# Cluster masks made in two ways, and a separate step for turning the row maxima, in a routed-attention and feed-forward kernel

## The chip, the core and the metric

The kernel runs on one core of a Trainium2 chip. A core has a matrix engine (TensorE, PE in the profile; its weight loads are the row PEld), a vector engine (VectorE, DVE), an activation engine (ScalarE, ACT), a general engine (GpSimd, POOL) and DMA queues. Here transfers are issued by the SyncE queue (SP) and, for one load, by ScalarE's own queue. Matrix products land in PSUM, which the tile framework hands out as banks; vector and scalar engines read them from there. Each engine takes its own instructions in order and waits for others by semaphores.

The metric is the device time of one execution in microseconds (us), the median of several runs.

## What is computed

Two blocks follow each other. In the first, each query and each key of a head is assigned to the nearest of 16 centroids (by cosine), and a query attends only to keys of its own cluster. The second is a feed-forward block with the activation `h * erf(softplus(h))`.

```python
# B, H, S, D = 4, 8, 768, 64 ; 16 clusters ; d_model 512, d_ff 2048 ; all float32
q_n = q / (norm(q) + 1e-6); k_n = ...; c_n = ...
q_assign = argmax(q_n @ c_n.T)            # the first maximum wins
k_assign = argmax(k_n @ c_n.T)
mask   = q_assign[..., :, None] == k_assign[..., None, :]
scores = where(mask, q @ k.T / sqrt(D), -1e9)
attn   = softmax(scores)
x      = attn @ v                          # then (B,H,S,D) -> (B*S, H*D)
h      = x @ w_in
out    = (h * erf(softplus(h))) @ w_out
```

## The kernel before

Heads are worked on in pairs: 16 pairs, four to a batch. Pair `p` has 12 score blocks of 128 keys by 384 queries for both heads; a block is called a slot below. While pair `p` goes through its slots, pair `p+1` is prepared beside it by a generator, `aside(p+1)`, which is advanced by single steps. The steps of a pair are: transpose q and k (VectorE); products with the centroids (`psim`) and half of the bf16 copies; the cluster choice (`hot`); the other bf16 copies; the masks; and then, for each half of the queries, a bf16 pass over all scores for the row maxima (`sm`, reduced to `nmx`), their minimum (`nm`), and the turning of these maxima into one row per head.

The masks are not a separate operand. They are rows of the bf16 operands `qm` and `km` that carry q and k as well, so that a second, bf16 product adds to the float32 scores a very negative number wherever clusters differ; the turned maxima are one more row of `qm`.

```python
# route(p), after the centroid products
ve.transpose(out=sims, in_=psim)
ve.reduce_max(out=mx, in_=sim, axis=AX.X)
ve.tensor_tensor(out=hot..., in0=sim, in1=mx (broadcast), op=ALU.is_equal)   # bf16, ties possible
ve.transpose(out=hotT, in_=hot)
yield
vectors("k")                       # bf16 copies of k, ScalarE
yield
won = ps_x.tile([P, HW], F32, name="won", tag="x")
te.matmul(won, lhsT=first, rhs=hotT, start=True, stop=True)   # subtracts earlier winners: first maximum only
for half in range(2):
    for e in range(2):
        if half == 0:
            ve.tensor_scalar(out=low["q"][r, e, cols], in0=won[g], scalar1=own[g, e:e+1], scalar2=0.0, op0=ALU.mult, op1=ALU.max)
        else:
            ae.activation(out=low["q"][r, e, cols], in_=won[g], func=ACT.Relu, scale=own[g, e:e+1])
        ae.activation(out=low["k"][r, e, cols], in_=won[g'], func=ACT.Identity, bias=nbig[g'], scale=BIG)
yield
# ... shift(p): six steps of sm and nmx, the last of them with the minimum, then
ve.tensor_reduce(out=nm, in_=nmx[:, :, ts], axis=AX.X, op=ALU.min)
yield
te.transpose(out=pn, in_=nm..., identity=identb)
ae.copy(out=nmT, in_=pn)
for e in range(2):
    for t in range(HJ):            # 6 rows, one transfer each, all on the SyncE queue
        nc.sync.dma_start(out=st["qm"][r:r+1, e, ...], in_=nmT[e*HJ+t : e*HJ+t+1])
yield
```

`ps_x`, the pool of PSUM banks that nearly everything shares (`psim`, `won`, `sm`, `pn`, `av`, `psum`, `hp`, `po`), has four buffers; the scores have two of their own.

The weights come in as 8-byte numbers and are converted on the chip, in 32 steps of two halves each: `convert()` is advanced by `prepare(n)`. The first half of a step has a maximum on VectorE and a sign pass on ScalarE; the second half has a shift on VectorE, an addition on GpSimd, and `split`, two ScalarE passes that open the next step.

The first batch goes by a fixed plan, one row for each of a pair's 12 slots:

```python
# (own steps, next pair's steps before the scores, after the scores, prepare)
plan = (
    (1,0,1,0), (1,0,2,0), (1,0,1,0), (1,0,0,0), (0,0,1,1), (0,0,1,1),
    (0,0,2,1), (0,0,2,1), (0,1,0,2), (0,1,0,0), (0,0,2,1), (0,0,1,1),
)
advance(0, 3); prepare(2); advance(0, NJ + 1); prepare(1); advance(0, HJ)   # before slot 0
for slot in range(48):
    advance(p, own_steps); advance(p + 1, before); scores([slot])
    ...divide, advance(p + 1, after), prepare(ops), accumulate(slot - 1), attend(slot - 2)
    if slot >= 45: pump(...)               # from here feed-forward products fill in
```

Engines keep program order up to slot 45. In the later batches scores go two slots at a time, the feed-forward products of the batch before (`hp`, `po`) are pumped between them, and the next pair's steps are taken at the places listed in `ASIDE`.

Of the kernel before, what the change touches and what calls it, by code (L numbers as in the profile page):

```python
# [8 lines left out]
F32 = mybir.dt.float32  # L9
BF16 = mybir.dt.bfloat16  # L10
# [3 lines left out]
ALU = mybir.AluOpType  # L14
ACT = mybir.ActivationFunctionType
AX = mybir.AxisListType
PSUM = bass.MemoryType.PSUM

P = 128
B, H, S, D = 4, 8, 768, 64  # L20
C = 16
NJ = S // P
Q = 32
NB = S // Q
HW = S // 2
HJ = NJ // 2
HP = H // 2
# [10 lines left out]
BIG = 2.0**60  # L38
FLOOR = 2.0**50
EPS = 2.0**-70  # L40
SH = 2 * C
# [2 lines left out]
SLOTS = 5  # L44


ASIDE = (*range(5), *range(8, 8 + 2 * NJ), 10 + 2 * NJ, 12 + 2 * NJ)
REST = 3
FIRST = 2 * NJ * HP - 3

# [18 lines left out]
def kernel(  # L69
# [10 lines left out]
    nc = tc.nc  # L80

    in_order = [True]
    te, ve, ae, ge = (
        InOrder(tc, e, in_order) for e in (nc.tensor, nc.vector, nc.scalar, nc.gpsimd)
    )
# [4 lines left out]
    const = pool("const", 1)  # L90
# [3 lines left out]
    routep = pool("routep", 1)  # L94
    small = pool("small", 2)
# [6 lines left out]
    ps_x = pool("ps_x", 4, space=PSUM)  # L102

    ident = const.tile([P, P], F32, name="ident")
    identb = const.tile([P, P], BF16, name="identb")
    minus = const.tile([P, D], F32, name="minus")
    first = const.tile([P, P], BF16, name="first")
    nbig = const.tile([P, 1], F32, name="nbig")
    ccT = const.tile([P, HP, 2 * C], F32, name="ccT")
# [2 lines left out]
    own = const.tile([P, 2], F32, name="own")  # L112
# [12 lines left out]
    pairs = {}  # L125
# [43 lines left out]
    for base, pattern, sign, op, fill in (  # L169
# [5 lines left out]
            out=first, in_=first, compare_op=op, fill=fill, base=base, pattern=pattern,  # L175
# [93 lines left out]
    for it in range(2):  # L269
# [4 lines left out]
            out=twice, in0=ss, scalar=inv, in1=norm, op0=ALU.mult, op1=ALU.add  # L274
# [3 lines left out]
            out=norm, in0=twice, scalar1=0.5, scalar2=(1e-6 if it else 0.0),  # L278
            op0=ALU.mult, op1=ALU.add,
# [11 lines left out]
    def route(p):  # L291
        st = pairs[p]
        low = lows[p % 2]
        for e in range(2 if p > 1 else 0):
            r = e * D + SH
            nc.sync.dma_start(out=low["q"][r : r + 1, e], in_=low["q"][r + 1 : r + 2, e])
        for nm in "qk":
            raw = rowp.tile([P, S], F32, name=nm + "T")
            ve.transpose(out=raw, in_=st.pop(nm).rearrange("p n t -> p (n t)"))
            st[nm + "T"], st[nm + "m"] = raw, low[nm]  # L300
        load_qk(p + 1)
        yield

        psim = ps_x.tile([P, HW], F32, name="psim", tag="x")
        for g in range(4):
            te.matmul(
                psim[2 * C * g : 2 * C * (g + 1)], lhsT=ccT[:, p % HP],
                rhs=st["qk"[g // 2] + "T"][:, (g % 2) * HW : (g % 2 + 1) * HW],
                start=True, stop=True,
            )  # L310

        def vectors(nm):
            for e in range(2):
                ae.copy(
                    out=low[nm][(1 - e) * D : (2 - e) * D, e], in_=st[nm + "T"][e * D : (e + 1) * D]
                )

        vectors("q")
        yield

        sims = routep.tile([P, HW], F32, name="sims")
        ve.transpose(out=sims, in_=psim)
        n = HW // C
        sim = sims.rearrange("p (g c) -> p g c", c=C)
        mx = routep.tile([P, n], F32, name="mx")
        ve.reduce_max(out=mx, in_=sim, axis=AX.X)
        hot = routep.tile([P, HW], BF16, name="hot")
        ve.tensor_tensor(
            out=hot.rearrange("p (g c) -> p g c", c=C), in0=sim,
            in1=mx.unsqueeze(2).to_broadcast([P, n, C]), op=ALU.is_equal,  # L330
        )
        hotT = routep.tile([P, HW], BF16, name="hotT")
        ve.transpose(out=hotT, in_=hot)
        yield
        vectors("k")
        yield

        won = ps_x.tile([P, HW], F32, name="won", tag="x")
        te.matmul(won, lhsT=first, rhs=hotT, start=True, stop=True)

        for half in range(2):
            cols = slice(half * HW, (half + 1) * HW)
            for e in range(2):
                r = slice(e * D, e * D + Q)
                g = slice(half * Q, (half + 1) * Q)
                if half == 0:
                    ve.tensor_scalar(
                        out=low["q"][r, e, cols], in0=won[g], scalar1=own[g, e : e + 1], scalar2=0.0,
                        op0=ALU.mult, op1=ALU.max,
                    )  # L350
                else:
                    ae.activation(
                        out=low["q"][r, e, cols], in_=won[g], func=ACT.Relu, scale=own[g, e : e + 1]
                    )
                g = slice(D + half * Q, D + (half + 1) * Q)
                ae.activation(
                    out=low["k"][r, e, cols], in_=won[g], func=ACT.Identity, bias=nbig[g], scale=BIG
                )
        yield


# [1 line left out]
    def shift(p):  # L363


        st = pairs[p]
        nmx = maxima[p % 2]
        load(p, "v", v, vp)
        for h in range(2):
            ts = slice(h * HJ, (h + 1) * HJ)  # L370
            for t in range(h * HJ, (h + 1) * HJ):
                for half in range(2):
                    for e in range(2):
                        sm = ps_x.tile([P, HW], F32, name="sm", tag="x")
                        te.matmul(
                            sm, lhsT=st["qm"][:, e, t * P : (t + 1) * P],
                            rhs=st["km"][:, e, half * HW : (half + 1) * HW], start=True, stop=True,
                        )
                        ve.tensor_reduce(
                            out=nmx[:, e, t, half : half + 1], in_=sm, axis=AX.X, op=ALU.max, negate=True  # L380
                        )
                    if (t, half) != ((h + 1) * HJ - 1, 1):
                        yield
            nm = small.tile([P, 2, HJ], BF16, name="nm")
            ve.tensor_reduce(out=nm, in_=nmx[:, :, ts], axis=AX.X, op=ALU.min)
            yield
            pn = ps_x.tile([2 * HJ, P], BF16, name="pn", tag="x")
            te.transpose(out=pn, in_=nm.rearrange("p e t -> p (e t)"), identity=identb)
            nmT = small.tile([2 * HJ, P], BF16, name="nmT")
            ae.copy(out=nmT, in_=pn)  # L390
            for e in range(2):
                r = e * D + SH
                for t in range(HJ):
                    nc.sync.dma_start(
                        out=st["qm"][r : r + 1, e, h * HW + t * P : h * HW + (t + 1) * P],
                        in_=nmT[e * HJ + t : e * HJ + t + 1],
                    )
            yield

# [203 lines left out]
    def prepare(n):  # L605
        for _ in range(n):
            next(conv, None)
# [3 lines left out]
    def aside(p):  # L611
# [3 lines left out]


    plan = (
        (1, 0, 1, 0), (1, 0, 2, 0), (1, 0, 1, 0), (1, 0, 0, 0), (0, 0, 1, 1), (0, 0, 1, 1),
        (0, 0, 2, 1), (0, 0, 2, 1), (0, 1, 0, 2), (0, 1, 0, 0), (0, 0, 2, 1), (0, 0, 1, 1),
    )  # L620
    ready = {0: aside(0)}
    part = iter(())
# [1 line left out]
    def advance(p, n):  # L624
        for _ in range(n):
            next(ready[p])
# [5 lines left out]
    for e in range(2):  # L632
        ve.tensor_copy(
            out=ccT[e * D : (e + 1) * D, :, e * C : (e + 1) * C],
            in_=pct[e * D : (e + 1) * D].rearrange("d (r e c) -> d r e c", e=2, c=C)[:, :, e],
        )
    ve.tensor_copy(out=identb, in_=ident)
    ve.memset(minus, -1.0)
    ve.memset(nbig, -BIG)
    ve.memset(alleps, S * EPS)  # L640
    for t in maxima:
        ve.memset(t, FLOOR)

    for e in range(2):
        ve.reduce_sum(
            out=own[:, e : e + 1],
            in_=ident.rearrange("p (g x c) -> p x g c", x=2, c=C)[:, e], axis=AX.XY,
# [4 lines left out]
    advance(0, 3)  # L652
    prepare(2)
    advance(0, NJ + 1)
    prepare(1)
    advance(0, HJ)
    for slot in range(2 * NJ * HP):
        in_order[0] = slot < FIRST
        p, r = divmod(slot, 2 * NJ)
        if r == 0:  # L660
            ready[p + 1] = aside(p + 1)
        own_steps, before, after, ops = plan[r]
        advance(p, own_steps)
        advance(p + 1, before)
        scores([slot])
        if r % NJ == 2 and slot > 2:
            part = divide(slot - 3)
            next(part)
        advance(p + 1, after)
        if r % NJ == 3:  # L670
            next(part, None)
        if slot not in (FIRST - 1, FIRST):
            prepare(ops)
        if slot > 0:
            accumulate(slot - 1)
        if slot >= 2:
            attend(slot - 2)
        if slot >= FIRST:
            pump(4 * NFT * TB)
# [13 lines left out]
    for u in range(2 * NJ * HP, len(units), 2):  # L693
        p, half, j = units[u]
# [59 lines left out]
```

## Time and profile before

| | us |
|---|---|
| median of 3 runs (1229.11 to 1232.9) | 1229.4 |
| profiled span | 1227.9 |
| first exponential (slot 0) starts | 35.04 |
| exponential of slot 44 starts, the last before feed-forward products begin | 166.52 |
| PE busy (95% of the span) | 1162.6 |
| DVE busy (38%) | 471.8 |
| ACT busy (48%) | 589.4 |
| POOL busy (38%) | 460.8 |

The mean granted TensorE clock is 0.98 of full. "Busy" for PE counts overlapping, modelled ends of pipelined products, so 95% isn't 95% of the engine's peak; which stage is limited by what is read from the order of instructions and from the waits in that stage.

### The profile page before, as it was taken

To read this page: it belongs to the slowest core of one execution; us is meant where nothing else is said; L and a number is where in the kernel's file an instruction comes from. 1 tells how busy PE (TensorE), PEld (TensorE's weight loads), DVE (VectorE), ACT (ScalarE), POOL (GpSimd) and SP (SyncE) were. 2 spreads that over 40 slices of the span, in tenths; PEclk is the share of its full clock that TensorE was granted. 3 is DMA by queue.
4 is the path that set the end of the run, shared out by engine and by line. 5 is a ranking of instruction groups with operands and counts; after the bars stand their busy time and mean duration, and the time that the engine had idled before them with its cause. 6 is when DMAs were issued, how large, how long until landed. Compare 5 with 4: busy or idle time off the path is not lost.

```text
span 1227.9 us, 13280 instructions
## 1 busy us (share of the span) xinstructions
PE 1162.6 (95%) x4913; PEld 621.7 (51%) x4913; DVE 471.8 (38%) x887; ACT 589.4 (48%) x705; POOL 460.8 (38%) x466
## 2 busy tenths in 40 slices
PE   4888979899999989999999999999999999999998
PEld 1222236564444545465465455455456456576663
DVE  5677864443443442333243244343425112011121
ACT  4687776677333545183364455256264254032222
POOL 2477774445333433154243234234234343030200
PEclk8799999899999999999999999999999999999999
DMA  8544332122020201020200201002000000000000
GB/s 133 125 91 91 79 115 56 54 67 48 3 46 16 42 8 33 9 41 8 35 23 1 48 10 26 22 10 39 4 27 1 9 9 1 12 7 18 0 18 18
DMA packets 140753, 42.95 MB, mean 35 GB/s; under 512 B 133520, under 2 KB 133520, under 8 KB 140688
## 3 DMA queue, kind: packets, MB, share of 16 engines
q1 hardware_dynamic: 137552, 41.70, 15.4%
q10 hardware_dynamic: 3136, 0.39, 0.3%
q8 instruction: 39, 0.64, 0.2%
q14 instruction: 26, 0.21, 0.1%
HBM read 35.68 MB, written 6.29 MB: 34 GB/s over the span
## 4 chain that ended last, share of the span: by engine, by line
PE 73%; ACT 10%; DVE 7%; issue 7%; DMA 2%; POOL 1%; ACTq 0%; SPq 0%; DVEq 0%
PE po L60 25%; PE hp L60 22%; PE sc L60 13%; PE av L60 6%; PE sm L60 4%; ACT a_s L60 2%; ACT L60 2%; DVE nmx L60 2%; ACT km L60 1%; DVE den L60 1%; PE psim L60 1%; ACT inv L60 1%; DVE w_out L60 1%; ACT pr L60 1%; ACT qm L60 1%
## 5 line engine op out<-in xcount | busy, mean ns | idle before, releaser
L60 PE MATMUL hp<-xT,w_in 128*128 128x256 f32 x1536 | 388.0, 389 | 7.1 <-DVE xT L60 5.4
L60 PE MATMUL po<-w_out,g 128*128 128x512 f32 x768 | 368.8, 598 | 0.6 <-DVE den L60 0.6
L60 POOL TENSOR_TENSOR acc<-acc,pr 128x384 f32<-128x384 f32 x256 | 239.3, 965 | 313.3 <-ACT pr L60 313.3
L60 PEld LDWEIGHTS hp<-xT,w_in 128*128 128x128 f32 x1536 | 288.6, 193 | 130.1 <-issue 81.6
L60 ACT ACT_TABLE_LOAD x111 | 142.4, 1283 | 231.3 <-DVE g L60 129.8
L60 DVE TENSOR_REDUCE nmx<-sm 128x1 f32<-128x384 f32 x384 | 195.5, 549 | 134.7 <-PE sm L60 133.8
L60 ACT ACTIVATE pr<-sc 128x768 f32<-128x768 f32 x192 | 148.0, 806 | 164.6 <-PE sc L60 164.0
L60 PEld LDWEIGHTS po<-w_out,g 128*128 128x128 f32 x768 | 142.0, 190 | 106.5 <-issue 93.6
L60 PE MATMUL sc<-qT,kT 64*128 64x384 f32 x768 | 186.5, 532 | 3.7 <-ACT pr L60 3.6
L60 POOL TENSOR_TENSOR g<-a_s,g 128x512 f32<-128x512 f32 x88 | 109.8, 1279 | 203.5 <-ACT a_s L60 203.5
L60 DVE COPY g<-hp 128x512 f32<-128x512 f32 x96 | 65.9, 687 | 282.1 <-PE hp L60 282.1
L60 PE MATMUL av<-pr,in_v 128*64 128x386 f32 x768 | 142.0, 500 | 0.8 <-DVE nmx L60 0.8
L60 PE MATMUL sm<-km,qm 128*128 128x384 bf16 x384 | 106.3, 341 | 31.8 <-DVE nmx L60 14.1
L60 PEld LDWEIGHTS sc<-qT,kT 64*128 64x128 f32 x768 | 71.6, 189 | 83.6 <-issue 47.2
L60 POOL TENSOR_TENSOR acc<-pr,pr 128x384 f32<-128x384 f32 x64 | 64.3, 1026 | 106.1 <-ACT pr L60 106.1
L60 PEld LDWEIGHTS av<-pr,in_v 128*64 128x64 f32 x768 | 49.5, 137 | 90.4 <-issue 76.8
L60 PEld LDWEIGHTS <-qm 128*128 128x128 bf16 x384 | 35.4, 99 | 95.2 <-issue 83.7
L60 DVE SCALAR_TENSOR_TENSOR den<-psum,inv 128x384 f32<-128x384 f32 x32 | 17.8, 556 | 141.5 <-ACT inv L60 141.2
L60 ACT ACTIVATE a_s<-a_s 128x2048 f32<-128x2048 f32 (+3 forms) x48 | 62.0, 1307 | 12.0 <-DMA a_s<-in_moe_w_out_dram 9.5
L60 PE MATMUL sc<-qm,km 64*128 64x384 bf16 x384 | 60.5, 326 | 2.8 <-DMA qm<-nmT 2.8
L60 ACT ACTIVATE a_s<-g 128x2048 f32<-128x2048 f32 x24 | 45.8, 1910 | 34.0 <-DVE g L60 33.8
L60 ACT ACTIVATE km<-won,nbig 32x384 bf16<-32x384 f32 x64 | 36.7, 574 | 36.2 <-DVE qm L60 35.5
(65 smaller groups left out, 530.6 us busy)
## 6 DMA issues: line engine op xcount, KB each, us to landing
w_out<-in_moe_w_in_dram SPq DMA_DIRECT2D x16, 512.0 KB, 4.1
in_q<-in_q_dram SPq DMA_DIRECT2D x64, 96.0 KB, 3.1
in_v<-in_v_dram SPq DMA_DIRECT2D x32, 192.0 KB, 3.1
out_dram<-osb SPq DMA_DIRECT2D x24, 256.0 KB, 2.0
in_k<-in_k_dram SPq DMA_DIRECT2D x60, 96.0 KB, 3.4
a_s<-in_moe_w_out_dram SPq DMA_DIRECT2D x8, 512.0 KB, 3.4
w_out<-in_moe_w_out_dram SPq DMA_DIRECT2D x8, 512.0 KB, 3.4
qm<-nmT SPq DMA_DIRECT2D x192, 0.2 KB, 1.7
```

The source lines that it names most:

```text
L60: ins = getattr(self.engine, name)(*args, **kw)
```

## The change

It has four parts.

1. **Masks of the first batch (pairs 0 to 3).** The product with `first` is cut into two 64-by-64 products, for queries and for keys, into two PSUM banks. ScalarE makes the four key masks first; VectorE makes two query masks and ScalarE the last two. The purpose is that the two engines needn't take turns at one bank.
2. **Masks of the later pairs (4 to 15).** No product and no PSUM: the equalities are multiplied by a rank (16 for the first centroid down to 1, times 2^60 for keys), the maximum is taken once more, and a comparison (queries) or a subtraction (keys) leaves one winner per row. Queries are then scaled by VectorE and keys copied by ScalarE, from bf16 in SBUF. These pairs have one step more, which `ASIDE` gets a place for.
3. **The turning of the maxima** becomes a function `turn(p, h)`. In the first batch it is called at named places: before slot 0 (now after one more step of maxima), at slot 3 and at slot 9; in later pairs it remains a step of the generator. The first pair's first turn issues its second three transfers on ScalarE's queue.
4. **The plan**: the half conversion step of slot 4, the slot of the masks, moves to slot 2.

```diff
+    rank = const.tile([P, C], F32, name="rank")
...
+        yield from (choose if p < HP else choose_later)(p, sim, mx, hot, hotT, low, vectors)
+    def choose(...):                          # first batch; hot and its transpose as before
-        won = ps_x.tile([P, HW], F32, name="won", tag="x")
-        te.matmul(won, lhsT=first, rhs=hotT, start=True, stop=True)
+        won = {}
+        for nm, r in (("q", slice(0, D)), ("k", slice(D, P))):
+            won[nm] = ps_x.tile([P, HW], F32, name="won" + nm, tag="x")[r]
+            te.matmul(won[nm], lhsT=first[r, r], rhs=hotT[r], start=True, stop=True)
+        # four Identity activations from won["k"], then per half and head from won["q"]:
+        #   half 0 on VectorE (mult, max), half 1 on ScalarE (Relu)
...
+    def choose_later(...):
+        ve.tensor_tensor(out=sim, in0=sim, in1=mx (broadcast), op=ALU.is_equal)
+        yield; vectors("k"); yield
+        ve.tensor_tensor(out=sim, in0=sim, in1=rank (broadcast), op=ALU.mult)
+        ve.reduce_max(out=mx, in_=sim, axis=AX.X)
+        for r, op in ((slice(0, D), ALU.is_equal), (slice(D, P), ALU.subtract)):
+            ve.tensor_tensor(out=hot[r]..., in0=sim[r], in1=mx[r] (broadcast), op=op)
+        ve.transpose(out=hotT, in_=hot)
+        yield
+        for half in range(2):
+            for e in range(2):
+                ve.tensor_scalar_mul(out=low["q"][r, e, cols], in0=hotT[g], scalar1=own[g, e : e + 1])
+                ae.copy(out=low["k"][r, e, cols], in_=hotT[g'])
+        yield
...
+            st["nm", h] = nm
+            if p >= HP:
+                yield
+                turn(p, h)
             yield
+    def turn(p, h):                           # transpose, copy and six transfers as before, but
+                queue = nc.scalar if (p, h, e) == (0, 0, 1) else nc.sync
...
-        (1, 0, 1, 0), (1, 0, 2, 0), (1, 0, 1, 0), (1, 0, 0, 0), (0, 0, 1, 1), (0, 0, 1, 1),
-        (0, 0, 2, 1), (0, 0, 2, 1), (0, 1, 0, 2), (0, 1, 0, 0), (0, 0, 2, 1), (0, 0, 1, 1),
+        (1, 0, 1, 0), (1, 0, 2, 0), (1, 0, 1, 1), (0, 0, 0, 0), (0, 0, 1, 0), (0, 0, 1, 1),
+        (0, 0, 2, 1), (0, 0, 2, 1), (0, 1, 0, 2), (0, 0, 0, 0), (0, 0, 2, 1), (0, 0, 1, 1),
...
+    for c in range(C):
+        ve.memset(rank[0:D, c : c + 1], float(C - c))
+    ve.tensor_scalar_mul(out=rank[D:P], in0=rank[0:D], scalar1=BIG)
...
     advance(0, NJ + 1)
+    turn(0, 0)
     prepare(1)
-    advance(0, HJ)
+    advance(0, HJ - 1)
...
+        if r == 3:
+            turn(p, 1)
+        elif r == 9 and p + 1 < HP:
+            turn(p + 1, 0)
```

(Cut: brackets and slices written out in full, and the place 6 added to `ASIDE`.)

## The prediction

> **What bounds the kernel now.** I read the page's slices first. Their columns are 40 equal slices of the span (30.7 us each), a digit being the busy share in tenths.
>
> ```profile
> PE   4888979899999989999999999999999999999998
> DVE  5677864443443442333243244343425112011121
> ACT  4687776677333545183364455256264254032222
> ```
>
> After about slice 10 TensorE shows 9 nearly everywhere: by the table of stretches it is busy 892 of the 908 us from 320 us to the end. There a saving must be TensorE work or a TensorE wait. In the first six slices it shows 4 to 9 while VectorE and ScalarE stand at 4 to 8: no engine is full, and the stage is set by chains between engines that keep program order. Feed-forward products come only from slot 45 on, after 170 us, so whatever shortens this stage should bring everything behind it forward by as much.
>
> Next I read the order of time. The exponentials of slots 0, 12, 24 and 36 start at 35.04, 70.41, 104.71 and 139.00: a prologue of 35 us, then about 34.3 us for a pair. Within a pair one gap is much the widest, after slot 4, where the masks are made. These are ScalarE's lines there (start, duration, operation, output and input, count, idle time before):
>
> ```profile
> 80.52 0.81 ACT L60 ACTIVATE pr<-sc 128x768 f32<-128x768 f32 x1 [0.28 <-PE sc L60]
> 81.37 0.57 ACT L60 ACTIVATE km<-won,nbig 32x384 bf16<-32x384 f32 x1
> 82.62 0.57 ACT L60 ACTIVATE km<-won,nbig 32x384 bf16<-32x384 f32 x1 [0.68 <-DVE qm L60]
> ...
> 84.99 0.57 ACT L60 ACTIVATE km<-won,nbig 32x384 bf16<-32x384 f32 x1
> 85.58 1.23 ACT L60 ACTIVATE w_out<-w_out 128x512 f32<-128x512 f32 x2
> 86.84 0.81 ACT L60 ACTIVATE pr<-sc 128x768 f32<-128x768 f32 x1
> ...
> 93.63 0.81 ACT L60 ACTIVATE pr<-sc 128x768 f32<-128x768 f32 x1 [2.00 <-PE sc L60]
> ```
>
> The exponential of slot 5 (86.84) waits behind six masks, one of them held up 0.68 us by VectorE, and behind the two passes of a weight conversion. VectorE in the same time:
>
> ```profile
> 80.73 0.60 DVE L60 TENSOR_SCALAR qm<-won,own 32x384 bf16<-32x384 f32 x1 [1.04 <-PE won L60]
> 81.98 0.61 DVE L60 TENSOR_SCALAR qm<-won,own 32x384 bf16<-32x384 f32 x1 [0.64 <-ACT km L60]
> ...
> 86.29 1.11 DVE L60 TENSOR_SCALAR w_out<-w_out 128x512 f32<-128x512 f32 x1 [2.13 <-ACT w_out L60]
> 87.33 1.94 DVE L60 TENSOR_REDUCE nmx<-sm 128x1 f32<-128x384 f32 x4
> ```
>
> It takes turns with ScalarE at the one bank `won`, then stands 2.13 us until ScalarE reaches that conversion, and only then reduces maxima. TensorE's `sm` product at 87.92 waits 1.83 us for those reductions, since its banks aren't free.
>
> The end of the prologue, from the timeline of all engines:
>
> ```profile
> 28.31 0.26 ACT L60 COPY nmT<-pn 6x128 bf16<-6x128 bf16 x1 [4.62 <-PE pn L60]
> 28.63 3.76 SPq L394 DMA_DIRECT2D qm<-nmT  x6
> 31.68 0.50 PE L60 MATMUL sc<-qm,km 64*128 64x384 bf16 x1 [0.45 <-DMA qm<-nmT]
> 34.52 0.48 PE L60 MATMUL sc<-qm,km 64*128 64x384 bf16 x1 [2.35 <-DMA qm<-nmT]
> 35.04 0.81 ACT L60 ACTIVATE pr<-sc 128x768 f32<-128x768 f32 x1 [5.79 <-PE sc L60]
> ```
>
> Six transfers leave one queue in 3.76 us (0.63 each); the second head's product waits 2.35 us for the last of them, and the first exponential 5.79 us.
>
> Last, who waited for instructions that touch `won`, over the whole run:
>
> ```profile
>   ACT km L60: 35.5, 23
>   DVE qm L60: 32.9, 32
>   PE sm L60: 5.8, 8
> ```
>
> The first two are idle time of ScalarE and VectorE; TensorE loses only 5.8 us here, 3.9 of it in the prologue. So the 35 us can't be counted as gain.
>
> [...] the first VectorE and ScalarE masks [...] alternate, 0.64 and 0.68 us of waiting each. Two banks remove that. [...] `hot`[...] takes 0.558 us at the median and 1.567 at most. [...]
>
> **The change part by part.**
>
> *Prologue.* Masks now run from 15.73 to 20.56 us. With two banks, ScalarE can start at about 15.8 and has six at 0.59 (their pitch where nothing waits), 3.5 us, to 19.3: 1.2 us earlier. The conversion behind them, and the maxima behind that (22.09 now), move by as much. Calling the turn after one more step of maxima also takes away VectorE's 0.46 us wait for the first product after it: about 0.4. Splitting the transfers makes three issues of one queue (1.9 us) the limit instead of six, so the second head's product needn't wait 2.35 us: the first exponential should start near 31 us. Not all 4 us are passed on, because what follows hangs on VectorE, which is then only 1.6 us ahead: it transposes the next pair until about 32.8 instead of 34.29. But there it now waits 1.18 us for an `sm` product stuck behind the late score product, and this goes. Centroid products can follow at about 32.9 and their transpose (37.69 now) at about 34.4: 3.3 us earlier. Against it, 16 memsets of 0.06 us and one scaling, some 1.2 us of VectorE, lie where it idles 0.97 us: 0.2 lost. **Sum: 3.1 us.**
>
> *Each pair of the first batch.* From the first mask to the last, ScalarE goes from 4.19 us to 3.54: 0.65. The conversion's two passes (1.23) leave the mask slot but enter slot 2, and between the exponentials of slots 2 and 4 ScalarE is as busy, idle only 0.28 us, so they merely move and are no gain by themselves. What gains is behind them: VectorE's maximum in slot 5 finds its input ready, the 2.13 us wait goes, the reductions come some 2 us earlier and TensorE's 1.83 us wait mostly goes. The slot-8 exponential waits 2.00 us for TensorE, the end of that chain, so 2 us is the ceiling and 0.65 the floor. Two mask banks leave one free bank fewer just then, which may cost TensorE 0.5 us. I choose 1.3 for each of the four pairs (the fourth prepares pair 4 by the later form: four ScalarE copies at 0.52, the duration of `inv`, the nearest plain pass over 384 columns, instead of 4.19 us). **Sum: 5.2 us.**
>
> *Later pairs.* `won` starts at 406.98 and the next product at 407.24: 0.26 us of TensorE, 12 times, 3.1 us. Once an `hp` product waits 0.9 us at 415.77 until ScalarE gives up `won`'s bank; such waits go, about 1. ScalarE saves 6 x 0.57 - 4 x 0.52 = 1.3 us a pair and waits less, off the path. VectorE gains a multiplication (0.56), a reduction (0.55), a second comparison of half the partitions (0.56) [...]: 1.5 us more a pair, 18 us in all, on an engine with about a third of its time used there. It comes as one block of nearly 4 us that can keep `hp` banks from being emptied; I charge 1.5. **Sum: 2.6 us.**
>
> Total 3.1 + 5.2 + 2.6 = 10.9: **1218.5 us**.
>
> **Rivals.** *The mask slot isn't the limit.* A pair has the same work in it, and ScalarE runs at 0.7 in this stage; then pairs give 0.2 us each and the time is about 1223. For it: ScalarE is nearly gapless from slot 2 to slot 6. Against: the 2.00 us wait at slot 8. *VectorE becomes the bound in later pairs.* Then 18 us more of it return as waits of products for `nmx` and `g`, say a third, 6 us: about 1224. For it: `hot` already stretches to 1.567 us beside GpSimd, and there are two more such operations. Against: over the later stretches TensorE waits for VectorE only about 14 us of 1013. *Banks are the real limit.* In the later pairs `won` holds one of four shared banks for some 5 to 9 us; free of it, TensorE could close more of its 16 us of holes: 1211. Against: only one wait names it.
>
> **Range and chances.** The prologue is surest (2 to 4 us); the pairs give 1 to 8 and the later pairs from 5 lost to 8 won, the more so as program order isn't kept there and a new order may help or hurt by itself. Together: 1209 to 1227. Faster by over 2% needs less than 1204.8, nearly all gains at their ceilings: 0.06. Slower by over 2% would need a new stall of 35 us: 0.01.
>
> **What would show each step.** First exponential near 31 us; slots 12, 24 and 36 behind it by about 33 us each; no alternation of masks; the slot-44 exponential (166.52) near 158.5; `nmx` after the masks without the 2.13 us wait; in later pairs fewer TensorE holes and no longer `hp` waits. I'd be wrong if the pair period stays at 34.3, or if the stage from slot 45 ends no earlier relative to its start because its order changed.

## Result and the profile after

The changed kernel takes 1211.89 us at the median of four runs (1207.0 to 1215.52), the kernel before 1229.67 beside it: a ratio of 0.9848, 95% interval 0.9806 to 0.9889, so 17.8 us less. The prediction said 10.9 less. The result lies inside its range; its terms are off, and the experiments were made to find out which of them failed.

From the page of the changed kernel, the rows of the slices that were shown of before, and with them the row of TensorE's granted clock (tenths of full speed; 30.1 us a slice here):

```profile
PE   4898989989999989999999999999999999999998
DVE  6777885645343535345263345335354112111121
ACT  4877775776434555272564346164265163122222
PEclk7998989899999999999999999999999999999999
```

The picture is the same: TensorE full after the first stages, below it until then, and in those stages a clock that isn't always granted in full. To see where the time went I cut the profiled execution at four marks: the first exponential, that of slot 44 (where program order stops being kept), the copy of the first output tile, and that of the 13th. The "clock loss" beside a length is that length times (1 - granted clock).

| stretch | before, us | clock loss | after, us | clock loss | predicted change | change |
|---|---|---|---|---|---|---|
| to the first exponential | 35.0 | | 31.4 | | -4, of which 3.1 are passed on | -3.6 |
| slots 0 to 44 | 131.5 | 5.8 | 131.7 | 10.1 | about -5 | +0.3 |
| slot 44 to first tile | 135.6 | 5.1 | 130.8 | 5.1 | none named | -4.9 |
| first to 13th tile | 586.2 | 5.1 | 572.0 | 0.0 | -2.6, with the last row | -14.2 |
| 13th tile to the end | 339.5 | 0.1 | 339.4 | 0.0 | | -0.2 |

(The profiled execution of after is its fastest: its span is 22.6 us shorter than that of before, against 17.8 between the medians.) One row came out as predicted. The pairs of the first batch brought nothing here, the stretch behind them brought something nobody had named, and the later pairs brought several times their term.

### The profile page after: what moved, and what is told of

It reads as the page before. It is cut to its first block, busy times and chain, and to the rows that moved or that the text cites. A ratio compares the mean times of both kernels' runs of the same rounds, so it can differ in the third digit from the quotient of the medians.

```text
span 1205.3 us, 13338 instructions
## 1 busy us (share of the span) xinstructions
PE 1151.6 (96%) x4905; PEld 617.0 (51%) x4905; DVE 515.9 (43%) x976; ACT 571.3 (47%) x680; POOL 461.7 (38%) x466
## 4 chain that ended last, share of the span: by engine, by line
PE 68%; issue 6%; ACT 3%; DVE 2%; DMA 0%; POOL 0%; ACTq 0%; SPq 0%; DVEq 0%; POOLq 0%
PE po L60 25%; PE hp L60 23%; PE sc L60 10%; PE av L60 6%; PE sm L60 3%; ACT L60 1%; PE psum L60 1%; ACT inv L60 1%; PE psim L60 1%; DVE den L60 1%; ACT a_s L60 0%; DVE xT L60 0%; DVE sims L60 0%; PE pn L60 0%; ACT pr L60 0%
## 5 line engine op out<-in xcount | busy, mean ns | idle before, releaser
L60 PE MATMUL hp<-xT,w_in 128*128 128x256 f32 x1536 | 383.4, 386 | 2.7 <-DVE xT L60 1.9
L60 PE MATMUL sc<-qT,kT 64*128 64x384 f32 x768 | 182.1, 529 | 7.1 <-ACT pr L60 6.9
L60 DVE SCALAR_TENSOR_TENSOR den<-psum,inv 128x384 f32<-128x384 f32 x32 | 17.8, 556 | 124.5 <-ACT inv L60 124.2
L60 ACT ACTIVATE a_s<-g 128x2048 f32<-128x2048 f32 x24 | 45.9, 1910 | 33.9 <-DVE g L60 31.8
L60 ACT ACTIVATE w_out<-w_out 128x512 f32<-128x512 f32 (+2 forms) x72 | 48.4, 704 | 6.5 <-DMA qm<-nmT 2.0
```

Of the source, the lines that this page charges most:

```text
L60: ins = getattr(self.engine, name)(*args, **kw)
```

## Reading the stages of the changed kernel

**Prologue.** The timeline of all engines, after (start, duration, operation, count, idle time before and what ended it):

```profile
15.10 2.36 ACT L60 ACTIVATE km<-wonk,nbig 32x384 bf16<-32x384 f32 x4 [2.19 <-PE wonk L60]
15.14 1.24 DVE L60 TENSOR_SCALAR qm<-wonq,own 32x384 bf16<-32x384 f32 x2 [0.48 <-PE wonk L60]
...
26.67 1.88 ACTq L442 DMA_DIRECT2D qm<-nmT  x3
26.71 2.91 SPq L442 DMA_DIRECT2D qm<-nmT  x3
...
30.86 0.50 PE L60 MATMUL sc<-qm,km 64*128 64x384 bf16 x2 [2.12 <-DMA qm<-nmT]
...
31.41 0.81 ACT L60 ACTIVATE pr<-sc 128x768 f32<-128x768 f32 x1 [2.04 <-PE sc L60]
```

VectorE and ScalarE start their masks together and neither waits for the other; the turn's transfers leave 2.0 us earlier (26.67 against 28.63). But the split did little: three issues take 2.91 us on SyncE's queue (0.97 each) and 1.88 on ScalarE's (0.63 each), where one queue alone took 0.63 each, and a product still waits 2.12 us for them.

**Slot 5.** The same place as in the prediction, in pair 1. ScalarE first, then VectorE, then TensorE, from their timelines:

```profile
74.22 1.49 ACT L60 ACTIVATE pr<-sc 128x768 f32<-128x768 f32 x2
75.73 2.35 ACT L60 ACTIVATE km<-wonk,nbig 32x384 bf16<-32x384 f32 x4
78.11 1.16 ACT L60 ACTIVATE qm<-wonq,own 32x384 bf16<-32x384 f32 x2
79.29 0.81 ACT L60 ACTIVATE pr<-sc 128x768 f32<-128x768 f32 x1
```

```profile
73.97 1.25 DVE L60 TENSOR_SCALAR qm<-wonq,own 32x384 bf16<-32x384 f32 x2 [0.59 <-PE wonk L60]
76.72 0.56 DVE L60 TENSOR_REDUCE nmx<-sm 128x1 f32<-128x384 f32 x1 [1.50 <-PE sm L60]
78.49 0.56 DVE L60 TENSOR_REDUCE nmx<-sm 128x1 f32<-128x384 f32 x1 [1.22 <-PE sm L60]
...
81.83 1.95 DVE L60 TENSOR_REDUCE nmx<-sm 128x1 f32<-128x384 f32 x4 [1.80 <-PE sm L60]
```

```profile
76.36 0.32 PE L60 MATMUL sm<-km,qm 128*128 128x384 bf16 x1 [0.21 <-ACT km L60]
78.13 0.32 PE L60 MATMUL sm<-km,qm 128*128 128x384 bf16 x1 [1.45 <-ACT km L60]
```

The six masks are gapless, 75.73 to 79.27: 3.54 us, to the hundredth what the prediction had. VectorE's 2.13 us wait for ScalarE's conversion is gone as well. In its place VectorE waits for TensorE: 1.50, 1.22 and 1.80 us. The second `sm` product shows why. It starts at 78.13, just behind the fourth key mask (75.73 + 2.35 = 78.08), and is named as waiting for it; the masks that a product reads were there after the second. What it waits for is the bank: `wonk` is given back only after its fourth reading. That is the free bank fewer, put at 0.5 us in the prediction.

What such a hole is followed by, from the table of stretches of after, a microsecond each (busy time of TensorE, its weight load, VectorE, ScalarE, GpSimd; then the granted clock, the share of the DMA engines and GB/s):

```profile
77.00:78.00 1.00, 0.00 (x0) 0.00 (x0) 0.28 (x1) 0.99 (x2) 1.00 (x3) 1.00 0.01 0
78.00:79.00 1.00, 0.87 (x5) 0.20 (x4) 0.51 (x2) 0.96 (x3) 1.00 (x2) 0.96 0.03 1
79.00:80.00 1.00, 1.00 (x4) 0.51 (x4) 1.00 (x2) 0.98 (x2) 0.74 (x1) 0.50 0.68 157
80.00:81.00 1.00, 1.00 (x6) 0.15 (x2) 0.03 (x1) 0.87 (x2) 0.00 (x0) 0.50 1.01 227
81.00:82.00 1.00, 1.00 (x7) 0.38 (x4) 0.17 (x1) 0.52 (x1) 0.00 (x0) 0.50 0.25 34
82.00:83.00 1.00, 0.99 (x5) 0.25 (x5) 1.00 (x3) 1.00 (x3) 0.00 (x0) 0.83 0.76 172
83.00:84.00 1.00, 1.00 (x8) 0.38 (x6) 1.00 (x3) 0.41 (x1) 0.00 (x0) 1.00 0.69 283
```

After the hole TensorE is busy without a gap, but at half clock for 3.4 us (0.04 + 0.50 + 0.50 + 0.50 + 0.17 = 1.71 us of clock lost). That is one **clock dip**, and the losses of the table come in such portions: 5.1 is three of them, 10.1 about six.

## The experiments

Each ran beside the kernel before on the same chip; the ratio is to that. The lengths are of the profiled executions.

| kernel | median, us | ratio (95%) | first exp. | slots 0-44 (loss) | to first tile (loss) | to 13th tile (loss) |
|---|---|---|---|---|---|---|
| before | 1229.67 | | 35.0 | 131.5 (5.8) | 135.6 (5.1) | 586.2 (5.1) |
| after | 1211.89 | 0.9848 (0.9806-0.9889) | 31.4 | 131.7 (10.1) | 130.8 (5.1) | 572.0 (0.0) |
| later_only | 1216.56 | 0.9891 (0.9860-0.9922) | 34.4 | 128.8 (6.2) | 135.5 (1.7) | 576.4 (5.1) |
| first_only | 1230.45 | 0.9995 (0.9980-1.0011) | 31.9 | 127.0 (3.8) | 143.2 (8.5) | 585.9 (5.1) |
| one_bank | 1205.49 | 0.9805 (0.9776-0.9833) | 32.2 | 130.4 (8.7) | 131.6 (1.7) | 573.3 (1.7) |
| plan_back | 1203.21 | 0.9790 (0.9759-0.9821) | 32.2 | 126.7 (3.4) | 131.1 (5.1) | 571.7 (0.0) |
| one_bank_plan | 1206.01 | 0.9804 (0.9774-0.9834) | 31.9 | 127.2 (5.7) | 131.9 (3.4) | 573.2 (1.7) |
| pair4_later | 1220.15 | 0.9919 (0.9888-0.9949) | 31.8 | 128.9 (5.5) | 131.0 (1.7) | 586.2 (5.1) |
| bank_brief | 1210.03 | 0.9830 (0.9801-0.9858) | 31.9 | 130.2 (5.1) | 130.3 (3.4) | 577.0 (1.7) |
| bank_held | 1209.81 | 0.9833 (0.9800-0.9866) | 32.0 | 125.8 (3.6) | 128.7 (0.0) | 578.1 (1.7) |
| turn_other_queue | 1226.89 | 0.9966 (0.9952-0.9979) | 32.4 | 128.3 (7.0) | 138.6 (7.0) | 587.6 (6.6) |
| one_change | 1227.67 | 0.9964 (0.9941-0.9987) | 32.1 | 133.7 (8.5) | 133.7 (5.1) | 592.3 (10.2) |
| dve_more | 1214.65 | 0.9868 (0.9839-0.9897) | 32.4 | 128.9 (7.2) | 132.3 (5.1) | 580.9 (6.8) |
| one_queue | 1207.04 | 0.9819 (0.9793-0.9845) | 32.7 | 126.3 (5.0) | 132.2 (1.7) | 576.4 (5.1) |

### One part of the change alone

My theory was that the two parts add up: the first batch's masks and turn would bring most, the later pairs a little.

**later_only** is the kernel before with the later pairs' part alone:

```diff
-    won = ...; te.matmul(won, lhsT=first, rhs=hotT); eight masks from won   # pairs 4-15
+    choose_later(...)                                                       # pairs 4-15
```

> The kernel before with part 2 alone: pairs 4 to 15 get their masks by rank and second maximum, without product and PSUM; the first batch, the turning and the plan stay as before. Theory A (most of the gain is in the later pairs, because TensorE is full there and the product, its bank and the clock dips after its holes are what was removed): about 1219, 9 to 12 us below before. Theory B (the prediction's split): 2.6 us below, about 1227. Both expect the first exponential at about 35 us.

**first_only** is the changed kernel with that part undone (and `ASIDE` as before):

```diff
-        yield from (choose if p < HP else choose_later)(...)
+        yield from (choose if p < HP else choose_old)(...)      # one product, one bank, as before
```

> The changed kernel with part 2 undone: pairs 4 to 15 make their masks by the product in one bank as before. Theory A: about 1223, 6 us below before, of which 3.6 in the prologue. Theory B: 8.3 us below, about 1221, with the pairs of the first batch at 33 us. The two differ more in the trace than in the time: A expects slots 12 to 24 and 24 to 36 at 35 to 36 us.

By the ratios (1 minus the ratio, of some 1230 us) later_only brings 13.4 us, first_only 0.6, which is nothing by its interval, and both together 18.7. The parts don't add up, and their sizes are the reverse of mine. Yet first_only is not idle: it stands 3.1 us ahead of before at the first exponential and 7.6 ahead at slot 44 (158.93 against 166.52), and has nothing left at the first tile (302.11 against 302.15). So it isn't that the masks were off the path: something between slot 44 and the first tile took it back.

Some of it is clock loss, 8.5 us in this stretch against 5.1. What else took it, from the timeline of SyncE's queue in first_only:

```profile
177.31 4.40 SPq L443 DMA_DIRECT2D qm<-nmT  x6
181.82 0.51 SPq L210 DMA_DIRECT2D w_out<-in_moe_w_out_dram  x1
```

and of ScalarE there:

```profile
177.19 0.78 ACT L60 ACTIVATE w_out<-w_out 128x512 int16<-128x512 f32 x1
185.43 2.06 ACT L60 ACTIVATE w_out<-w_out 128x512 f32<-128x512 f32 x3 [7.46 <-DMA w_out<-in_moe_w_out_dram]
```

The first turn of pair 4 stands in the queue until its maxima are turned; by the waits of that queue it stood there 7.9 us. Behind it, in the same queue, stands the last of six loads of `w_out`, and ScalarE waits 7.46 us for that load before it can go on converting weights. In the changed kernel the order on the queue is another:

```profile
160.86 19.38 SPq L210 DMA_DIRECT2D w_out<-in_moe_w_out_dram  x6
181.30 4.22 SPq L442 DMA_DIRECT2D qm<-nmT  x6
```

All six loads are ahead of the turn; the queue waits 1.0 us for the maxima and ScalarE at most 1.5 us for a load. The two kernels differ here in the form of pair 4 alone, and the later form has one step more in its preparation. It moves the turn one step back in an order that is no longer the program's.

### Is it pair 4's place in the queue?

**pair4_later** is first_only with the later form for pair 4 alone:

```diff
-        yield from (choose if p < HP else choose_old)(...)
+        yield from (choose if p < HP else choose_later if p == HP else choose_old)(...)
```

> The changed kernel with the old product masks in pairs 5 to 15 only; pair 4 keeps the later form. Theory A (the first batch's gain was lost after slot 44, because with pair 4's steps one earlier its turn stands before weight loads in the transfer queue and ScalarE waits 7.5 us for such a load): that wait goes, the gain of about 8 us at slot 44 is still there at the first output tile, and the time is about 1220. Theory B (the gain is always lost there, whatever the order, since the stretch after slot 44 is bound by weights and conversion): first output tile near 302 as before, time about 1229.

It takes 1220.15 against 1230.45. From slot 44 to the first tile it needs 131.0 us instead of 143.2, and ScalarE waits at most 0.9 us for `w_out`. So one pair's form out of twelve brings 9 us by the ratios. (In the profiled executions the stretch differs by 12 us, but 6.8 of these are clock loss.) The rival, that the whole second part is a saving spread over the pairs, holds for the rest of it only.

**turn_other_queue** leaves the form of first_only and takes pair 4's first turn out of that queue:

```diff
-                queue = nc.scalar if (p, h, e) == (0, 0, 1) else nc.sync
+                queue = nc.scalar if (p, h, e) == (0, 0, 1) or (p, h) == (HP, 0) else nc.sync
```

> The run with part 2 undone, but the six transfers of pair 4's first turn are issued on ScalarE's queue, so that the weight load behind them in SyncE's queue need not stand until the maxima are turned (7.9 us there). If that order is what ate the first batch's gain after slot 44: the load leaves some 4 us sooner, ScalarE's 7.5 us wait for it shrinks to under 4 (it pays about 3.6 us for the issuing itself), and the first output tile comes 2 to 5 us before 302, the time being about 1226 to 1228. If the stretch is bound otherwise: 1230 again.

ScalarE's longest wait for `w_out` falls from 7.5 to 3.6 us, the stretch from 143.2 to 138.6, the ratio from 0.9995 to 0.9966 (3.6 us; the intervals don't meet). So the queue is a cause, but not the whole of it: about 6 us against pair4_later stay, by the ratios. In the 3.6 us that stay ScalarE isn't only waiting: it issues the six transfers itself, for 3.73 us, until 0.5 us before the load is there.

Nor is the form of pair 4 a protection by itself. later_only has it with the plan of before, which takes one step more of pair 4 at slot 45. Counted in steps, before takes pair 4's first turn at slot 45, first_only and later_only as the first step behind the scores of slot 46, after and pair4_later as the second. later_only's queue is that of first_only:

```profile
161.20 12.03 SPq L210 DMA_DIRECT2D w_out<-in_moe_w_out_dram  x5
179.35 3.89 SPq L430 DMA_DIRECT2D qm<-nmT  x6
183.36 1.32 SPq L210 DMA_DIRECT2D w_out<-in_moe_w_out_dram  x1
```

and ScalarE waits 7.8 us for `w_out` there (3.4 in before). So two kernels with different forms and the same place of the turn have the same wait: the place decides it. What costs the rest stays open. ScalarE's waits for the loads that follow (`a_s`) sum to 18.6 us in first_only and 19.3 in turn_other_queue against 11.8 in pair4_later, and the clock loss is larger there too (8.5 and 7.0 against 1.7).

### The first batch: two banks, and the moved conversion

**one_bank** is the changed kernel with one product into one bank for pairs 1 to 3; VectorE's two masks come first, then ScalarE's six, so that the engines change over only once:

```diff
-        for nm, r in (("q", slice(0, D)), ("k", slice(D, P))):
-            won[nm] = ps_x.tile(...)[r]
-            te.matmul(won[nm], lhsT=first[r, r], rhs=hotT[r])
+        both = ps_x.tile([P, HW], F32, name="won", tag="x")          # pairs 1-3
+        te.matmul(both, lhsT=first, rhs=hotT)
+        # two q masks on VectorE, four k masks and two q masks on ScalarE
```

> The changed kernel, but in pairs 1 to 3 both halves of the product stand in one bank again, with VectorE's two query masks first and then ScalarE's six, so that the engines change over once. Theory A (the second mask bank keeps an sm product waiting for a bank, 1.45 us in slot 5, and the TensorE clock dips after it): that wait goes, slots 12 to 24 and 24 to 36 fall to about 33 us, and the time falls by 3 to 5 us to about 1208. Rival (the sm product waits for the key masks as data, not for the bank): nothing is won, and ScalarE, starting no later, leaves the time within 1 us of the changed kernel.

**plan_back** is the changed kernel with the half step of the weight conversion back in slot 4, where it was before the change:

```diff
-        (1, 0, 1, 0), (1, 0, 2, 0), (1, 0, 1, 1), (0, 0, 0, 0), (0, 0, 1, 0), (0, 0, 1, 1),
+        (1, 0, 1, 0), (1, 0, 2, 0), (1, 0, 1, 0), (0, 0, 0, 0), (0, 0, 1, 1), (0, 0, 1, 1),
```

> The changed kernel with the half conversion step back in slot 4, the slot of the masks. If moving it to slot 2 brings something (VectorE's maximum in slot 5 then finds its input ready), each pair of the first batch gets 1 to 2 us longer, 3 to 6 us in all, about 1216. If the move only shifts ScalarE's two passes from one full stretch to another, within 1 us of the changed kernel.

**one_bank_plan** has both edits.

> Both mendings of the first batch in one kernel: pairs 1 to 3 with one mask bank and VectorE first, and the half conversion step back in slot 4. If the bank wait and the shifted step are separate costs, pairs take about 32.5 us and the time is about 1201; if the gain of the plan was only that it took the strain off the same slot 5, it is within 2 us of the changed kernel with the old plan (1203).

In one_bank the wait at slot 5 is gone. From its timeline, pair 1:

```profile
80.41 2.37 ACT L60 ACTIVATE km<-won,nbig 32x384 bf16<-32x384 f32 x4
...
81.03 0.32 PE L60 MATMUL sm<-km,qm 128*128 128x384 bf16 x1 [0.21 <-ACT km L60]
...
81.63 0.32 PE L60 MATMUL sm<-km,qm 128*128 128x384 bf16 x1 [0.27 <-ACT km L60]
```

The second `sm` product follows 0.60 us behind the first, not 1.77, while the same four masks are still running: it has a bank. That shows the 1.45 us as a wait for a bank and not for data. By the medians one_bank is 6 us faster than after and plan_back 9, and together they do not add up (1206.01). All three medians lie below the fastest run of after (1207.0), but the intervals of the ratios overlap with after's, so that a gain on the changed kernel is likely and not shown. plan_back is the best version that ran, faster than the kernel before by 2.1% (1.8 to 2.4).

How much of this lies in slots 0 to 44? The table warns against reading one profile there. after, pair4_later and one_change have the same program up to slot 44 and need 131.7, 128.9 and 133.7 us, with clock losses of 10.1, 5.5 and 8.5. Means are little better: before and later_only 130.1; after and the four others with its first batch 129.9; plan_back and the four others with its masks and plan 127.6. Their clock losses have means of 6.0, 7.0 and 4.8, so nearly all of the 2.3 us between the last two are clock loss.

A cleaner measure is the time for twelve slots, from the exponential of slot 12 to that of 24 and from there to that of 36, taken only where no dip falls into it:

| first batch as in | kernels | twelve slots without a dip, us |
|---|---|---|
| before | before, later_only | 34.2 to 34.4 (all four), mean 34.3 |
| after | after, first_only, pair4_later, turn_other_queue, one_change | 34.0 to 34.3 (six of ten), mean 34.1 |
| plan_back | plan_back, bank_brief, bank_held, dve_more, one_queue | 33.6 to 33.8, once 34.2 (all ten), mean 33.7 |
| one_bank | one_bank | 33.2 and 33.4 |
| one_bank_plan | one_bank_plan | 33.7 and 33.7 |

So the first batch of after gains 0.2 us in each of these two pairs where 1.3 was forecast, that of one_bank 0.8 more, and the conversion put back 0.4 more. The other four of after's ten have a dip and take 35.0 to 36.2. In each of the ten, `sm` waits 1.45 us for the bank, and the four dips begin within 1.5 us of that wait; in the eighteen of the other rows there is no dip (in plan_back the wait is 0.97 us). So the second bank costs twice here: by the wait, and by the dips that come with it in some executions. The length of a hole alone doesn't decide: the four of before and later_only each have one of 1.8 us and no dip.

### One queue for the first turn

**one_queue** is plan_back without the split:

```diff
-                queue = nc.scalar if (p, h, e) == (0, 0, 1) else nc.sync
+                queue = nc.sync
```

> The changed kernel with the old plan, and the first pair's six turned maxima all on SyncE's queue again. The prediction's step: the second head's product waits for the last of six transfers, the first exponential comes at about 33.5 instead of 32.2, and since the next pair hangs on VectorE less of it is passed on: about 1 us in the time, 1204.

The first exponential starts at 32.72 instead of 32.17, and slot 44 at 159.01 instead of 158.87. Splitting six issues over two queues was worth 0.55 us at the first exponential and nothing measurable by slot 44; the times' intervals overlap.

### The later pairs: bank, product, VectorE, alternation

From the first to the 13th tile, where the eight pairs 7 to 14 are prepared, TensorE is the bound (busy 575.1 of 586.2 us in before, 564.1 of 572.0 in after) and one profile can be trusted once the clock loss is taken off (the clean stretch below). The five kernels with the old form there (before, first_only, pair4_later, turn_other_queue, one_change) have 581.1, 580.8, 581.1, 581.0 and 582.1; the six with the later form as changed (after, later_only, one_bank, plan_back, one_bank_plan, one_queue) 572.0, 571.3, 571.6, 571.7, 571.5 and 571.3. The later form thus brings 9.6 us in eight pairs, 1.2 a pair. later_only against before shows it with no correction at all: both lose 5.1 us of clock, and the stretch goes from 586.2 to 576.4.

Part of the clock loss goes with the form as well. It is 6.5 us on average in the five and 2.3 in the six. One dip is in all five at the same place, 259 to 263 us behind the first tile (562.12 in before), and in none of the nine kernels with the later form. From the timeline of TensorE in before, just ahead of it:

```profile
559.25 0.32 PE L60 MATMUL sm<-km,qm 128*128 128x384 bf16 x1 [0.58 <-DVE den L60]
560.63 0.70 PE L60 MATMUL hp<-xT,w_in 128*128 128x256 f32 x2 [1.06 <-DVE xT L60]
```

These two holes are gone with the later form, and the dip with them.

Where the 9.8 us lie, by TensorE's groups in this stretch, before:

```profile
L60 PE MATMUL hp<-xT,w_in 128*128 128x256 f32 x690 | 179.6, 391 | 3.0 <-DVE xT L60 2.1 <-ACT km L60 0.9
L60 PE MATMUL sc<-qT,kT 64*128 64x384 f32 x408 | 102.4, 522 | 3.7 <-ACT pr L60 3.6
L60 PE MATMUL won<-hotT,first 128*128 128x384 bf16 x8 | 2.6, 326 | 0.0
```

and later_only:

```profile
L60 PE MATMUL hp<-xT,w_in 128*128 128x256 f32 x690 | 179.5, 391 | 0.0
L60 PE MATMUL sc<-qT,kT 64*128 64x384 f32 x408 | 100.0, 524 | 4.8 <-ACT pr L60 4.7
```

The products' counts agree, so the same work is compared. The eight `won` products are gone (2.6 us); so are the waits of `hp` for `xT` and `km` (3.0), and one of `sm` for `den` (1.2), while `sc` waits 1.1 us more; by the table of stretches the idle time falls by 3.3 us in all, and the busy time by 6.5. Of the latter 3.9 us are left when `won` is taken off, 2.4 of them in `sc` at the same count; what they are stays open.

**bank_brief** is plan_back with the product put back in pairs 4 to 15, read at once by a one-column copy of VectorE; **bank_held** reads it with a copy of ScalarE after its last mask, meant to keep the bank taken as long as in the kernel before:

```diff
+        won = ps_x.tile([P, HW], F32, name="won", tag="x")
+        te.matmul(won, lhsT=first, rhs=hotT, start=True, stop=True)
+        seen = small.tile([P, 1], F32, name="seen")
+        ve.tensor_copy(out=seen, in_=won[:, 0:1])      # bank_held: ae.copy, after the masks
```

> The changed kernel with the old plan, and in pairs 4 to 15 the product is made again beside the later form, into a shared bank which VectorE reads at once by one tiny copy. It costs TensorE 0.26 us a pair, 3 us in all, and holds the bank for about a microsecond. If the product's own time is what mattered in the later pairs: 1206 to 1207, 3 us above 1203. If it is the bank held long: within 1.5 us of that.

> As the run with the brief bank, but the bank is read by ScalarE after its last mask copy, so that it is held for as long as the masks take, as in the kernel before. If holding one of four shared banks is the larger part of what the later pairs lost: 1211 to 1215, 8 to 12 us above 1203. If banks don't matter: the same as with the brief bank, about 1206.

They are slower than plan_back by 6.8 and 6.6 us at the median; in the clean stretch by 3.6 and 4.7 (575.3 and 576.4 against 571.7). But bank_held doesn't hold the bank as it was meant to. From the product's start to the end of its last reading before needs 5.2 to 8.7 us in each of the eight pairs of this stretch, bank_held 4.9 in one and 0.5 to 2.0 in the other seven: in six of the eight the product starts only after ScalarE's last mask. So the rival "banks are the real limit" stays untested in the later pairs. The product itself costs more than its own 2.6 us, since there are waits with it. From the waits of bank_brief's TensorE in that stretch:

```profile
PE won L60 <- DVE den L60: 1.5, 3, 0.6
PE sm L60 <- DVE den L60: 1.0, 1, 1.0
```

These are waits (total, times, longest) that the changed kernel's TensorE doesn't have there. So the product, put back, costs about 3.6 of the 9.6 us; the other 6 belong to the long-held bank, the other masks and the order that came with them, which these runs don't separate.

**one_change** asks whether it was the alternation of the two engines at the bank. It is pair4_later with VectorE's two masks first and ScalarE's six behind them in pairs 5 to 15:

```diff
-    for half ...: for e ...: q mask (VectorE or ScalarE); k mask (ScalarE)
+    for half ...: for e ...: q masks of half 0 (VectorE)
+    then ScalarE: four k masks, two q masks
```

> The run with the old product masks in pairs 5 to 15, but there VectorE makes its two query masks first and ScalarE its six after them, so that the engines change over at the bank once, not four times. If the alternation at one bank was a good part of what the later pairs lost: 3 to 4 us below that run's 1220, about 1216. If it was off the path, as the few TensorE waits say: 1219 to 1221.

It isn't faster: 0.9964 against 0.9919 (its 20 runs spread from 1219.9 to 1236.7 us), and 582.1 against 581.1 us in the clean stretch. The alternation was off the path in later pairs.

**dve_more** asks what VectorE's additional work costs; it is plan_back with three reductions more in each later pair, which repeat one that is there (3 x 0.55 = 1.65 us):

```diff
         ve.reduce_max(out=mx, in_=sim, axis=AX.X)
+        for _ in range(3):
+            ve.reduce_max(out=mx, in_=sim, axis=AX.X)
```

> The changed kernel with the old plan, and in pairs 4 to 15 three more reductions of 0.55 us each on VectorE beside the later form, 1.65 us a pair, 20 us in all, about as much as the later form itself added. My prediction charged 1.5 us for such an addition: about 1205. If VectorE's work in the later pairs is free: 1203. If a third of it comes back as waits: 1210.

The median rises by 11.4 us for 20 us of work. Of its profile, 2.4 us lie in the clean stretch after the clock loss is taken off (574.1 against 571.7, for 13.2 us of added work), and 6.8 are the clock loss itself, four dips where plan_back has none. So VectorE's work isn't free in later pairs, between about a fifth (2.4 of 13.2) and three fifths (11.4 of 20) of it comes back; whether the dips belong to it or to chance, one profile can't say. The three reductions are half of what the later form itself added, not about as much: in the clean stretch VectorE is busy 222.1 us in before and 248.7 in later_only, 3.3 us more a pair.

## Why the prediction was right and wrong

**The prologue: right.** The first exponential was expected near 31 us and came at 31.41, 3.6 earlier (2.7 to 3.3 in the other kernels that have all of it); of this 3.1 was to be passed on, and the next pair's transpose of `psim` starts 3.6 earlier, at 34.06. The waits at the bank and the wait before the turn went as worked out. The term inside it for the split was too high: not 2.35 us of waiting removed but 0.55, as one_queue shows, and an issue on SyncE's queue took 0.97 us beside ScalarE's instead of 0.63.

**The pairs of the first batch: the term that failed.** "I choose 1.3 for each" gave 5.2; where no dip fell, each of the two middle pairs gained 0.2, and in after's profile dips took even that. Two steps of the working were wrong. "Two mask banks leave one free bank fewer just then, which may cost TensorE 0.5 us" was the larger: the `sm` product waits 1.45 us for that bank, four of ten such waits came with a half-clock dip, and in one_bank, without that wait, a pair takes 0.8 us less. And the conversion's two passes don't "merely move": put back, they leave a pair 0.4 us shorter. The statement that a pair's floor was 0.65 us took for granted that ScalarE's masks alone set the end of the chain; the 2.13 us wait went and came back as VectorE's 1.50, 1.22 and 1.80 us for TensorE. The rival "the mask slot isn't the limit" had the size right, 0.2 a pair.

**What was ahead at slot 44 was to be handed on whole** ("whatever shortens this stage should bring everything behind it forward by as much"). first_only refutes it: 7.6 us ahead at slot 44, none at the first tile. The prediction named the danger (program order isn't kept there, a new order may hurt or help by itself) but gave it no number; it was worth 9 us between first_only and pair4_later. Pair 4's added step kept the weights' last load ahead of a turn in the queue; moving that turn to another queue brings 3.6 of them, and the rest is open.

**The later pairs: right in kind, too small by a factor.** The term was 3.1 + 1 - 1.5 = 2.6 for twelve pairs. Measured, for eight: product 2.6, waits 3.3, and 3.9 of unsettled busy time, 9.8 in all with VectorE's charge already in it. The waits were mis-sized most: counting only the one wait that names `won`'s bank missed those of `hp` for `xT` (2.1 us) and of `sm` for `den` (1.2), which name VectorE's results. VectorE's addition was mis-sized too: the 1.5 us a pair in the working was my estimate, and 3.3 were measured. The later form has two half comparisons where the working counts one, and its four query masks take 0.52 us each on average in these eight pairs, where two took 0.61 each in before. The charge for it, 1.5 us in all, was too low by dve_more (2.4 in eight pairs for half of that work), which makes the gross gain larger still. In after's profile another 5.1 us come from three clock dips that aren't there; later_only and one_queue, with the same code in these pairs, have three each, so at most the one at 562 us can be booked to the change.

So it is luck that 1211.89 lies inside the range. The errors partly cancel: the pairs are 5 us short, the order behind slot 44 and the later pairs well over.

## What to carry to other kernels

Count a bank as taken until its last reader, and look whose next product needs it, before splitting one bank's work into two: here `sm` waited 1.45 us, until the fourth mask had been made from `wonk`. Where one queue carries both data that is waited for and weights that aren't, a step added or removed can change who stands behind whom (in first_only the turn stood 7.9 us, and ScalarE waited 7.46 us for the load behind it): mark the time at several points of the run, or a gain and a loss of 8 us look like nothing. And take the clock loss off a stretch before comparing two profiles, where TensorE is its bound; here that turned lengths of 571.7 to 576.4 us into values within 0.7 us of each other.

## What the runs showed of the hardware

The clock was lost in portions: in all fourteen profiles every loss between the prologue and 900 us is 1.7 us or a whole multiple of it. The 2.67 us hole in which TensorE waits for `pr` is in every kernel; in the kernel before, the table of stretches continues behind it like this:

```profile
448.00:449.00 1.00, 0.62 (x4) 0.30 (x4) 0.00 (x0) 1.00 (x3) 0.53 (x1) 1.00 0.00 0
449.00:450.00 1.00, 1.00 (x4) 0.64 (x3) 0.00 (x0) 0.44 (x1) 1.00 (x2) 0.74 0.03 8
450.00:451.00 1.00, 1.00 (x4) 0.80 (x3) 0.00 (x0) 0.00 (x0) 1.00 (x2) 0.50 0.00 0
451.00:452.00 1.00, 1.00 (x5) 0.35 (x3) 0.00 (x0) 0.00 (x0) 1.00 (x2) 0.50 0.00 0
452.00:453.00 1.00, 1.00 (x4) 0.53 (x6) 0.00 (x0) 0.00 (x0) 0.06 (x1) 0.55 0.00 0
453.00:454.00 1.00, 1.00 (x8) 0.55 (x5) 0.68 (x1) 0.47 (x1) 0.00 (x0) 1.00 0.00 0
```

and in after, behind the same hole, like this:

```profile
435.00:440.00 5.00, 2.33 (x11) 1.28 (x11) 0.69 (x1) 4.64 (x6) 1.29 (x2) 1.00 0.00 0
440.00:445.00 5.00, 4.94 (x25) 3.06 (x23) 2.97 (x5) 2.83 (x4) 4.21 (x6) 1.00 0.07 11
```

A dip is half clock for about 3.4 us and costs 1.7 us (0.26 + 0.50 + 0.50 + 0.45 here). Dips came with some holes and not with others of the same length: with four of the ten of 1.45 us in slots 12 to 36, and with the 2.67 us hole in eight of the fourteen kernels. What else decides isn't shown.

The query masks of the later form, a scaling of 384 elements of 32 partitions from bf16 to bf16 on VectorE, took 0.311 us at the median of 48 in after, and 1.234 at most. The long ones go with GpSimd: the 18 that took over 0.4 us each had a GpSimd instruction beside them and ended 0.11 or 0.12 us after its end; the 30 others took 0.307 to 0.313, and only one of them had a GpSimd instruction beside it, for 0.1 us.
